# Wider runs in the first transform stage: nine runs of 512 columns for the first four rows, five runs for two later rows

## The chip, the cores and the metric

The kernel runs on one core of a Trainium2 chip. The metric is the device time of one execution in microseconds (us), as the median of several runs. When single instructions ran and how long they took is read from one profiled execution, whose times count from the start of its span.

## What is computed

The reference applies four layers to x of 2048 positions by 576 columns. Layers one and three mix by two Fourier matrices, layers two and four convolve and gate:

```python
x = x + _A_ref(_layernorm(x), seq_re, seq_im, hid_re, hid_im)
x = x + _B_ref(_layernorm(x), B_k, B_v, B_shift_k, B_ssm_k, B_ssm_D)
# _A_ref: y = Cr @ (x @ Wr) - Ci @ (x @ Wi)
# _B_ref: kv = shift_conv(k) * v;  y = q * (long_conv(kv, ssm_k) + kv * ssm_D)
```

The long convolution of kv with ssm_k does not depend on x, and both convolution layers use the same one. It is computed once, in several transform stages, beside the first mixing layer.

## The kernel before, in words

All products are made in float32r from a high and a low part: ScalarE (ACT) copies a tile into its rounded high part (L99, in `split`), VectorE (DVE) subtracts to get the low part (L100), and three of the four products of parts are summed on TensorE (PE).

**The main line.** The function `layer` runs the first mixing layer in steps. A step loads one 128 x 512 block of the Fourier matrix, splits it (`load_c`, L99 and L100, tile mats<-flts; called a c split here), and makes 14 matmuls of 512 columns: 12 into four banks s0 to s3 and two into the bank rm, which stand last. So the place in the program can be told by counting pairs of rm matmuls: the pair number n closes step n-1. In the first sixteen steps normalised rows of x are made too, on ACT, DVE and GpSimd (POOL).

**The first transform stage** is the generator `branch` (L351). The 2048 positions are 16 rows j of 128 partitions. A row has two items of 576 columns: source 1 is ssm_k as loaded, source 0 is the product kv. Source 0 comes from `convolve` (L384): for two rows together, DVE makes the shift convolution with multiplies and adds of 128 x 1152 (L395, L400); then L428 multiplies a row of it by v. An item is then split into f1r (L99 on ACT, tile f1r<-f1f for source 0 and f1r<-flts for source 1; L100 on DVE). The rows 0 to 3 (`K_FIRST`) keep a tile for each item; from row 4 on the two items of a row share a tile of 1152 columns, in which halves of 288 columns of source 0 and source 1 alternate.

A **run** (`f1_products`, L443) takes a stretch of columns of one such tile and makes six matmuls with the stage's constants: three products of parts, each for the upper and for the lower 64 partitions, which go to two banks. The weights there are 64 x 128, those of the main line 128 x 128. Three PSUM banks bf0, bf1, bf2 are handed out in turn (`turn`, L80), so a run shares one bank with the run before it. Behind the six matmuls ACT copies the two banks out (L453, here an eviction), and then issues one DMA that stores both halves to the tensor td in DRAM (L454). Rows 0 to 3 are 8 items with two runs of 288 columns each, 16 runs; each later row is three runs of 384 (`VW`), 36 runs.

**What sets the order.** `visits` is the list of runs that are due, each with the half step of the generator from which it may be emitted; `visit` emits at most one at a time. The loop around `layer` calls the generator at a pace that a table of numbers gives (`F1_16`, `F1_END`). A scheduler then puts the instructions of all engines into an order by its own model. On the chip every engine works through its own order and never passes an instruction that waits. The next stage (`bk<-mid`, L454's td as input) begins after the first stage's last stores, in step 45.

Of the kernel before, what the change touches and what calls it, by code (L numbers as in the profile page):

```python
# [12 lines left out]
AF = mybir.ActivationFunctionType  # L13
# [3 lines left out]
HP = P // 2  # L17
S = 2048
D = 576
J = S // P  # L20
TB = 4
NT = 512
HD = D // 2
# [7 lines left out]
ROWS = (0, 1, 2, 3, 4, 5, 6, 7, 8, 9)  # L31
K_FIRST = 4
F1_16 = 5
VW = 384
F1_END = 42
W_FROM = 41
HOLD = 125
# [14 lines left out]
WIDE = 2 * NT  # L52
# [14 lines left out]
def fnet_h3_kernel(ctx: ExitStack, tc: tile.TileContext, x, c_mat, w_re, w_im, k_pad, v, shift_k,  # L67
# [7 lines left out]
    def mm(ps, lhsT, rhs, first, last, more=False):  # L75
        return nc.tensor.matmul(ps, lhsT, rhs, start=first, stop=last, skip_group_check=more).ins  # L76
# [3 lines left out]
    def turn():  # L80
        given[0] += 1
        return banks[(given[0] - 1) % 3]
# [61 lines left out]
    def two(v):  # L144
        return v.rearrange("p (a n) -> p a n", a=2)
# [79 lines left out]
    W = {}  # L225

    def load_w():
        lay(flts, SC_AT + CRAW * NT + 4 * D, ("wl", D, 3))
# [122 lines left out]
    def branch():  # L351
        f1r = region_b(FR, "f1r")
        lay(f1r, 0, ("xf", 2 * D, 4), ("fc", 2 * P, 5))
        lay(f1r, 0, ("xp", 4 * D, 2))
        at = lay(flts, SC_AT + CRAW * NT, ("so", D, 4), ("land", D, 3))
        lay(flts, SC_AT + CRAW * NT, ("sp", 2 * VW, 3))
        lay(flts, at, ("craw", NT, 1))
        f1f = region_a(F32, "f1f")
        ks = f1f[:, :KR * 2 * D]
# [80 lines left out]
            parted[:] = split(h, l, two(r))  # L440
            return tuple(paired)

        def f1_products(j, fc, xf, at, n, so, to):  # L443
            ps = [turn()[:, :n] for _ in range(2)]
            last = seq[-1:]
            for k, (a, b) in enumerate(((0, 1), (0, 0), (1, 0))):
                for i in (1, 0):
                    half = slice(i * HP, (i + 1) * HP)
                    with behind(*last):
                        last = [mm(ps[i], fc[half, a, :], xf[b][half, at:at + n], k == 0, k == 2)]  # L450
            so = two(ring[so]())
            for i in range(2):
                stored[:] = [nc.scalar.activation(so[:, i, :], ps[i], AF.Copy).ins]  # L453
            nc.scalar.dma_start(t_d[:, j::J, to:to + n], so)  # L454

        conv, made_ops, visits = convolve(), 0, []
# [4 lines left out]
        for n, (j, src) in enumerate(todo):  # L461
            f1_loads(n + 1)
            if n < 2:
                yield
            xf = f1_split(j, src)
            if j < K_FIRST:
                visits += [(2 * n + 2, j, fcs[j], xf, hf * HD, HD, "so", hf * D + src * HD) for hf in range(2)]
            elif src:
                visits += [(2 * n + 3, j, fcs[j], xf, at, VW, "sp", at) for at in range(0, 2 * D, VW)]
            if n:  # L470
                f1_loads(n + 3)
            later = [m for m in range(n + 1, len(todo)) if todo[m][1] == 0 and 7 * (todo[m][0] // 2 + 1) > made_ops]
            for half in range(2):
                visit(2 * n + half)
                if later and n > 2:
                    left = 7 * (todo[later[0]][0] // 2 + 1) - made_ops
                    for _ in range(-(-left // (2 * (later[0] - n) - half)) if left > 0 else 0):
                        next(conv)
                        made_ops += 1
                yield  # L480
# [695 lines left out]
```

## Time and profile before

| what | value |
|---|---|
| median of three runs | 1181.65 us (1181.65 to 1184.18) |
| the profiled execution's own time | 1182.72 us |
| its span | 1180.9 us |
| ACT, busy | 650.9 us, 55% |
| POOL, busy | 75.5 us, 6% |
| evictions bf (L453) | 104, 43.2 us |
| stores td (L454) | 52 |

The profiled execution's time is 1.8 us above its span; this part lies outside of the trace. In rows of the trace the first number is the start or the stretch, the second the busy time; what stands in brackets is idle time of the engine ahead of the instruction, and what ended it. A row of several instructions (x6) runs from the first start to the last end. The matmuls overlap, so their distance in time is read from starts and not from lengths.

### The profile page before, as it was taken

To read this page: it belongs to the slowest core of one execution; us is meant where nothing else is said; L and a number is where in the kernel's file an instruction comes from. 1 tells how busy PE (TensorE), PEld (TensorE's weight loads), DVE (VectorE), ACT (ScalarE), POOL (GpSimd) and SP (SyncE) were. 2 spreads that over 40 slices of the span, in tenths; PEclk is the share of its full clock that TensorE was granted. 3 is DMA by queue.
4 is the path that set the end of the run, shared out by engine and by line. 5 is a ranking of instruction groups with operands and counts; after the bars stand their busy time and mean duration, and the time that the engine had idled before them with its cause. 6 is when DMAs were issued, how large, how long until landed. Compare 5 with 4: busy or idle time off the path is not lost.

```text
span 1180.9 us, 18086 instructions
## 1 busy us (share of the span) xinstructions
PE 1168.1 (99%) x6198; PEld 990.1 (84%) x6198; DVE 868.5 (74%) x1564; ACT 650.9 (55%) x1280; POOL 75.5 (6%) x115
## 2 busy tenths in 40 slices
PE   8999999999999999999999999999999999999997
PEld 6776667988888988888888898888888888889997
DVE  7899983788877778777757765965776776775764
ACT  7865655577766667766645666534434445450210
POOL 2310000000000000001101111000000000001111
PEclk9999999999999999999999999999999999999999
DMA  9879898545666656648966776862872787795621
GB/s 330 291 230 310 263 299 279 170 152 170 209 215 200 201 170 192 185 144 246 271 188 221 243 247 228 260 236 76 259 244 72 229 288 247 258 329 160 214 92 41
DMA packets 147453, 255.64 MB, mean 216 GB/s; under 512 B 16161, under 2 KB 56353, under 8 KB 147362
## 3 DMA queue, kind: packets, MB, share of 16 engines
q1 hardware_dynamic: 111890, 210.17, 55.7%
q10 hardware_dynamic: 28560, 37.91, 9.1%
q0 software_dynamic: 6912, 6.43, 2.4%
q8 instruction: 48, 0.79, 0.3%
q14 instruction: 43, 0.35, 0.1%
HBM read 187.80 MB, written 66.65 MB: 215 GB/s over the span
## 4 chain that ended last, share of the span: by engine, by line
PE 86%; DVE 5%; ACT 3%; DMA 3%; issue 2%; SPq 0%; ACTq 0%; POOL 0%; DVEq 0%
PE s L76 49%; PE bk L76 30%; PE rm L76 5%; PE bf L76 2%; DMA flts<-in_c_mat 1%; ACT flts L514 1%; DVE f1f L395 1%; DVE f1f L400 1%; DVE mats L100 1%; ACT mid L514 1%; DVE mid L520 1%; DMA early<-in_x 0%; ACT mats L99 0%; DMA yb<-flts 0%; DMA flts<-td 0%
## 5 line engine op out<-in xcount | busy, mean ns | idle before, releaser
L76 PE MATMUL s<-mats 128*128 128x512 f32 x2102 | 547.0, 396 | 3.9 <-DVE mats L761 1.5
L76 PEld LDWEIGHTS s<-mats 128*128 128x128 f32 x2102 | 383.7, 189 | 85.9 <-issue 11.1
L100 DVE TENSOR_TENSOR mats<-flts,mats 128x512 fp32r<-128x512 f32 x206 | 140.6, 687 | 50.5 <-ACT mats L99 48.9
L99 ACT ACTIVATE mats<-flts 128x512 fp32r<-128x512 f32 x206 | 128.2, 627 | 82.1 <-PE bk L76 31.6
L76 PE MATMUL bk<-mid 128*128 128x288 f32 x704 | 126.6, 301 | 1.5 <-ACT flts L514 0.8
L76 PEld LDWEIGHTS bk<-mid 128*128 128x128 f32 x704 | 108.7, 188 | 21.9 <-ACT flts L514 5.7
L514 ACT ACTIVATE flts<-bk 128x288 f32<-128x288 f32 (+1 forms) x192 | 76.5, 405 | 91.1 <-PE bk L76 76.0
L76 PE MATMUL bk<-w,u 128*128 128x288 f32 x864 | 120.4, 296 | 0.0
L76 PEld LDWEIGHTS bk<-w,u 128*128 128x128 f32 x864 | 117.4, 188 | 2.9 <-ACT flts L514 0.9
L520 DVE TENSOR_TENSOR mid<-flts,mid 128x576 fp32r<-128x576 f32 (+1 forms) x149 | 93.3, 627 | 19.1 <-ACT mid L514 16.3
L76 PE MATMUL rm<-mats 128*128 128x512 f32 x304 | 94.6, 391 | 0.2 <-ACT flts L514 0.2
L514 ACT ACTIVATE mid<-flts 128x576 fp32r<-128x576 f32 (+1 forms) x148 | 80.5, 576 | 9.8 <-DVE flts L535 5.1
L289 DVE TENSOR_TENSOR flts<-flts,bk 128x288 f32<-128x288 f32 x48 | 21.8, 454 | 68.3 <-PE bk L76 68.3
L76 PE MATMUL bk<-mats 128*128 128x288 f32 (+1 forms) x376 | 67.9, 317 | 0.0
L76 PEld LDWEIGHTS rm<-mats 128*128 128x128 f32 x304 | 57.0, 188 | 12.6 <-ACT flts L514 0.6
L453 ACT ACTIVATE flts<-bf 128x384 f32<-128x384 f32 (+1 forms) x104 | 43.2, 462 | 42.6 <-PE bf L76 39.8
L76 PE MATMUL s<-t,mats 128*128 128x512 f32 x264 | 64.9, 389 | 0.0
L186 POOL TENSOR_TENSOR flts<-flts 128x1 f32<-128x1 f32 x34 | 28.0, 823 | 516.4 <-DVE flts L185 514.0
L76 PE MATMUL bk<-mats,t 128*128 128x288 f32 (+1 forms) x368 | 59.3, 303 | 0.0
L514 ACT ACTIVATE flts<-flts 64x288 f32<-64x288 f32 x128 | 56.7, 443 | 4.5
L76 PEld LDWEIGHTS bk<-mats 128*128 128x128 f32 x376 | 55.5, 188 | 3.4
L76 PEld LDWEIGHTS s<-t,mats 128*128 128x128 f32 x264 | 49.6, 188 | 10.3
(152 smaller groups left out, 1495.5 us busy)
## 6 DMA issues: line engine op xcount, KB each, us to landing
flts<-in_c_mat SPq DMA_DIRECT2D x148, 256.0 KB, 3.6
ph<-in_c_mat SPq DMA_DIRECT2D x54, 512.0 KB, 4.1
flts<-in_c_mat SPq DMA_DIRECT2D x30, 512.0 KB, 5.7
flts<-td SPq DMA_DIRECT2D x53, 288.0 KB, 3.0
td<-flts ACTq DMA_DIRECT2D x36, 384.0 KB, 4.4
vd<-flts ACTq DMA_DIRECT2D x64, 144.0 KB, 2.5
flts<-vd SPq DMA_DIRECT2D x32, 288.0 KB, 3.9
ud<-ph ACTq DMA_DIRECT2D x12, 512.0 KB, 6.2
```

The costliest lines, as they stand in the source:

```text
L76: return nc.tensor.matmul(ps, lhsT, rhs, start=first, stop=last, skip_group_check=more).ins
L99: a = nc.scalar.activation(h, src, AF.Copy).ins
L100: return a, nc.vector.tensor_tensor(l, src, h.bitcast(F32), OP.subtract).ins
L186: pows.append(nc.gpsimd.tensor_tensor(rs, ve, mhalf, OP.pow).ins)
L289: added[:] = [nc.vector.tensor_tensor(r[:, cs], r[:, cs], ps[:, :HD], OP.add).ins]
L395: nc.vector.tensor_tensor(out_t[:, n], k, wt[3 - t][:, n], OP.mult)
L400: nc.vector.tensor_tensor(rp, rp, out_t, OP.add)
L453: stored[:] = [nc.scalar.activation(so[:, i, :], ps[i], AF.Copy).ins]
L514: last_act.append(nc.scalar.activation(*args, **kw).ins)
L520: nc.vector.tensor_tensor(l, src, h.bitcast(F32), OP.subtract)
```

## The change

Rows 0 to 3 no longer make two runs for each item. Their 8 x 576 columns are filled into runs of 512 one after the other, nine in all, and a run may so hold the end of one item and the start of the next (64 and 448, 128 and 384, and so on). For later rows two rows together, 2304 columns, make five runs of 464, 464, 464, 456 and 456; the third holds the last 224 columns of the even row and the first 240 of the odd row, which are of source 0 alone. A run that holds two pieces makes 12 matmuls, six for each piece, in the same two banks. The number of matmuls in the stage and the sum of their columns stay as they were; the number of runs goes from 52 to 39, that of the evictions from 104 to 78.

The stores change too. A store of rows 0 to 3 still takes both halves, but there is one for each piece and each half item: 24, not 16. In later rows each half is stored by itself, and each piece: 12 for two rows, not 6. Together 96, not 52. The output buffers become two of 1024 columns (so) and later five of 464 (sp) in place of four of 576 and three of 768. And the half steps at which runs are due change: an even row's first run is due one half step earlier.

```diff
-        def f1_products(j, fc, xf, at, n, so, to):
-            ps = [turn()[:, :n] for _ in range(2)]
-            last = seq[-1:]
+        def f1_products(pieces, so):
+            ps, last, at = [turn() for _ in range(2)], seq[-1:], 0
...
             for k, (a, b) in enumerate(((0, 1), (0, 0), (1, 0))):
-                for i in (1, 0):
-                    half = slice(i * HP, (i + 1) * HP)
-                    with behind(*last):
-                        last = [mm(ps[i], fc[half, a, :], xf[b][half, at:at + n], k == 0, k == 2)]
-            so = two(ring[so]())
+                for o, fc, xf, src, n in placed:
+                    for i in (1, 0):
+                        half = slice(i * HP, (i + 1) * HP)
+                        with behind(*last):
+                            last = [mm(ps[i][:, o:o + n], fc[half, a, :], xf[b][half, src:src + n],
+                                       k == 0 and o == 0, k == 2, o > 0)]
+            both = two(ring[so]()) if so == "so" else None
             for i in range(2):
-                stored[:] = [nc.scalar.activation(so[:, i, :], ps[i], AF.Copy).ins]
-            nc.scalar.dma_start(t_d[:, j::J, to:to + n], so)
+                one = ring[so]() if both is None else both[:, i, :]
+                stored[:] = [nc.scalar.activation(one[:, :at], ps[i][:, :at], AF.Copy).ins]
+                if both is None or i == 1:
+                    for (j, *_, to), (o, *_) in zip(pieces, placed):
+                        for n, cols in to:
+                            if both is None:
+                                nc.scalar.dma_start(t_d[:, j + i * J, cols:cols + n], one[:, o:o + n])
+                            else:
+                                nc.scalar.dma_start(t_d[:, j::J, cols:cols + n], both[:, :, o:o + n])
+                            o += n
...
-                visits += [(2 * n + 3, j, fcs[j], xf, at, VW, "sp", at) for at in range(0, 2 * D, VW)]
+                at, widths = (CUT[2], CUT[3:]) if j % 2 else (0, CUT[:2])
+                for i, w in enumerate(widths):
+                    visits.append((2 * n + 2 + j % 2 + i * (2 - j % 2), [(j, fcs[j], xf, at, w, [(w, at)])], "sp"))
+                    at += w
+                if at < 2 * D:
+                    open_run.append((j, fcs[j], xf, at, 2 * D - at, [(2 * D - at, at)]))
```

Line numbers of the changed kernel are higher: its evictions are L461, its stores L466 and L468, the high and low parts L100 and L101, the product with v L430, the convolution L397 and L402.

The scheduler's order moves at these places. The first is PE's order around its pair number 23 of rm matmuls, which ends step 22. Before, the last three runs ahead of it are those of row 4:

```order
L76 MATMUL bf1_67<-f1r_167 128x384
L76 MATMUL bf0_66<-f1r_167 128x384
L76 MATMUL s2_71<-mats_73 128x512 x3
L76 MATMUL s3_72<-mats_73 128x512 x3
L76 MATMUL rm_795<-mats_73 128x512 x2
L76 MATMUL s0_69<-mats_73 128x512
L76 MATMUL s1_70<-mats_73 128x512
```

Of the changed kernel, at the same pair of rm, with the last two matmuls of the run that joins rows 4 and 5 (224 and 240 columns) ahead of it, and the first two of row 5's run of 456 behind it:

```order
L77 MATMUL bf2_68<-f1r_167 128x240
L77 MATMUL bf1_67<-f1r_167 128x240
L77 MATMUL s0_69<-mats_73 128x512 x3
L77 MATMUL s1_70<-mats_73 128x512 x3
L77 MATMUL s2_71<-mats_73 128x512 x3
L77 MATMUL s3_72<-mats_73 128x512 x3
L77 MATMUL rm_790<-mats_73 128x512 x2
L77 MATMUL bf1_67<-f1r_167 128x456
L77 MATMUL bf0_66<-f1r_167 128x456
```

Ahead of this pair of rm stand 19 of the 52 runs before, and 12 of the 39 now. Of these 12, the first of row 4 (464 columns, both sources) stands 34 main matmuls and two more runs ahead of the end of the pair. The run of 456 writes bf1 first, which the joined run wrote too.

The second place is ACT's order there: the evictions of that joined run and what stands around them. Before, the item of row 6, source 0 (f1r<-f1f), stands ahead of the evictions of row 5's second run:

```order
L453 ACTIVATE flts_75<-bf0_66 128x384
L453 ACTIVATE flts_75<-bf2_68 128x384
L99 ACTIVATE mats_73<-flts_75 128x512
L454 DMA td_79<-flts_75 256x1x384
L99 ACTIVATE f1r_167<-f1f_168 128x2x288
L453 ACTIVATE flts_75<-bf1_67 128x384
L453 ACTIVATE flts_75<-bf2_68 128x384
```

In the changed kernel both items of row 6 stand ahead of the evictions (464 columns, bf2 and bf1) of the run that joins rows 4 and 5:

```order
L461 ACTIVATE flts_75<-bf0_66 128x464
L461 ACTIVATE flts_75<-bf2_68 128x464
L466 DMA td_79<-flts_75 128x464 x2
L100 ACTIVATE f1r_167<-f1f_168 128x2x288
L100 ACTIVATE f1r_167<-flts_75 128x2x288
L461 ACTIVATE flts_75<-bf2_68 128x464
L461 ACTIVATE flts_75<-bf1_67 128x464
L100 ACTIVATE mats_73<-flts_75 128x512
L466 DMA td_79<-flts_75 128x224
L466 DMA td_79<-flts_75 128x240
```

The two stores that end the piece come a second time, for the other half, and then the evictions of the run of 456. So ACT is now asked for row 6 ahead of the joined run's evictions, where it was asked ahead of those of row 5's second run before.

The third place is DVE's order just ahead of row 6's product with v. Before:

```order
L100 TENSOR_TENSOR f1r_167<-f1f_168,f1r_167 128x2x288
L395 TENSOR_TENSOR f1f_168<-f1f_168 128x1152
L100 TENSOR_TENSOR mats_73<-flts_75,mats_73 128x512
L100 TENSOR_TENSOR f1r_167<-flts_75,f1r_167 128x2x288
L400 TENSOR_TENSOR f1f_168<-f1f_168 128x1152
L100 TENSOR_TENSOR mats_73<-flts_75,mats_73 128x512
L428 TENSOR_TENSOR f1f_168<-f1f_168,flts_75 128x576
```

And of the changed kernel:

```order
L101 TENSOR_TENSOR f1r_167<-f1f_168,f1r_167 128x2x288
L397 TENSOR_TENSOR f1f_168<-f1f_168 128x1152
L101 TENSOR_TENSOR mats_73<-flts_75,mats_73 128x512
L101 TENSOR_TENSOR f1r_167<-flts_75,f1r_167 128x2x288
L402 TENSOR_TENSOR f1f_168<-f1f_168 128x1152
L397 TENSOR_TENSOR f1f_168<-f1f_168 128x1152
L430 TENSOR_TENSOR f1f_168<-f1f_168,flts_75 128x576
```

Counted from the end of step 15's evacuation (u<-flts) to this product, the changed order has one c split less and one operation of the convolution more; the rest of the operations are the same. Behind step 44 the orders of all engines agree.

More of the change, by code (lines that the diff above doesn't have):

```diff
@@ L227, in load_w @@
     def load_w():
-        lay(flts, SC_AT + CRAW * NT + 4 * D, ("wl", D, 3))
+        lay(flts, SC_AT + CRAW * NT + OUT_END, ("wl", D, 3))
         wg = region_a(FR, "w").rearrange("p (k n) -> p k n", k=9)
@@ L354, in branch @@
         lay(f1r, 0, ("xp", 4 * D, 2))
[L355 to L356 removed]
+        lay(flts, SC_AT + CRAW * NT, ("so", WIDE, 2))
+        at = lay(flts, SC_AT + CRAW * NT + OUT_END, ("land", D, 3))
+        lay(flts, SC_AT + CRAW * NT, ("sp", CUT[0], 5))
         lay(flts, at, ("craw", NT, 1))
@@ L466, in branch @@
             if j < K_FIRST:
-                visits += [(2 * n + 2, j, fcs[j], xf, hf * HD, HD, "so", hf * D + src * HD) for hf in range(2)]
-            elif src:
-                visits += [(2 * n + 3, j, fcs[j], xf, at, VW, "sp", at) for at in range(0, 2 * D, VW)]
+                at = 0
+                while at < D:
+                    w = min(NT - filled(), D - at)
+                    cut = [max(at, HD * hf) for hf in range(2)], [min(at + w, HD * (hf + 1)) for hf in range(2)]
+                    open_run.append((j, fcs[j], xf, at, w, [(hi - lo, lo % HD + hf * D + src * HD)
+                                                            for hf, (lo, hi) in enumerate(zip(*cut)) if lo < hi]))
+                    at += w
+                    if filled() == NT:
+                        visits.append((2 * n + 2, list(open_run), "so"))
+                        open_run.clear()
+            elif not src and j % 2:
+                open_run.append((j, fcs[j], xf, 0, CUT[2], [(CUT[2], 0)]))
+                visits.append((2 * n + 3, list(open_run), "sp"))
+                open_run.clear()
+            elif src:
+                at, widths = (CUT[2], CUT[3:]) if j % 2 else (0, CUT[:2])
+                for i, w in enumerate(widths):
+                    visits.append((2 * n + 2 + j % 2 + i * (2 - j % 2), [(j, fcs[j], xf, at, w, [(w, at)])], "sp"))
+                    at += w
+                if at < 2 * D:
+                    open_run.append((j, fcs[j], xf, at, 2 * D - at, [(2 * D - at, at)]))
             if n:
```

11 lines of the change are left out of this document (9 added, 2 removed).

## The prediction

> **What bounds the kernel now.** I read the page first, then the chain of work that ended last for the first 230 us, then the busy times in stretches of 20 us, then the timelines of PE, ACT and DVE where they meet.
>
> ```profile
> PE 1168.1 (99%) x6198; PEld 990.1 (84%) x6198; DVE 868.5 (74%) x1564; ACT 650.9 (55%) x1280; POOL 75.5 (6%) x115
> ```
>
> PE is busy all the time, so what shortens PE's own work should shorten the kernel, as long as PE doesn't wait. The chain says where it nearly does:
>
> ```profile
> 74.69 2.48 PE s L76 x10
> 78.34 1.27 DVE f1f L400
> ...
> 116.03 1.15 DVE f1f L400
> 117.44 1.13 issue
> 121.06 0.80 PE bf L76 x6
> ```
>
> From 78 to 117 us the chain runs over DVE's convolution and not over PE. In the stretches, the columns after the length are busy PE, PEld, DVE and ACT:
>
> ```profile
> 20.00:40.00 20.00, 20.00 (x99) 15.23 (x99) 17.13 (x46) 18.94 (x39) 3.78 (x5) 1.00 0.99 364
> 40.00:60.00 20.00, 20.00 (x96) 15.35 (x95) 17.55 (x35) 17.14 (x39) 6.89 (x4) 1.00 0.70 238
> 60.00:80.00 20.00, 20.00 (x100) 14.99 (x98) 18.86 (x28) 13.31 (x28) 2.58 (x4) 1.00 0.72 215
> 80.00:100.00 20.00, 20.00 (x103) 14.59 (x102) 20.00 (x24) 10.10 (x22) 1.58 (x3) 1.00 0.88 281
> 100.00:120.00 20.00, 20.00 (x102) 13.65 (x101) 20.00 (x24) 10.92 (x23) 1.06 (x2) 1.00 0.98 330
> ```
>
> DVE has no idle time at all from 80 to 120 us. The change takes nothing from DVE. So two engines bound this stage, and a gain on PE counts only where DVE has already delivered.
>
> **What a run costs PE.** The change makes fewer, wider runs with as many matmuls and columns. What a run costs beside its columns can be read from starts:
>
> ```profile
> 198.54 2.72 PE s L76 x12
> ...
> 78.46 0.68 PE L76 MATMUL bf<-f1r 64*128 64x288 f32 x6
> 79.07 0.96 PE L76 MATMUL s<-mats 128*128 128x512 f32 x3
> 79.95 0.66 PE L76 MATMUL bf<-f1r 64*128 64x288 f32 x6
> ...
> 146.88 0.79 PE L76 MATMUL bf<-f1r 64*128 64x384 f32 x6
> 147.60 1.66 PE L76 MATMUL s<-mats 128*128 128x512 f32 x6
> 149.19 0.79 PE L76 MATMUL bf<-f1r 64*128 64x384 f32 x6
> ```
>
> Twelve main matmuls in the chain take 2.72 us, 0.227 each. From one run of 288 to the next are 1.49 us with three main matmuls between (0.68), so the run costs 0.81. For 384 it is 2.31 less six (1.36), 0.95. The two widths differ by 3 x 96 columns (upper and lower halves run side by side) and by 0.14 us, 0.00049 us a column; so 0.39 us of each run is for getting into the 64-row weights and out again. Runs of 512, 464 and 456 then cost 1.14, 1.07 and 1.06.
>
> All runs of before: 16 x 0.81 + 36 x 0.95 = 47.2 us. After: 9 x 1.14 = 10.2; six pairs of rows at 3 x 1.07 + 2 x 1.06 = 5.33 each, 32.0. Short pieces add something that no row shows. At least it is nothing; at most a pair of matmuls waits for its weights, which come in three pairs in 0.43 us (row below), 0.14 a pair, where 64, 128 and 192 columns alone need 0.03, 0.06 and 0.09. For two pieces of each width and three products that is at most 1.4; I take 0.7, in the middle. One run of rows 0 to 3 is cut in two by main matmuls, 0.4. Sum 43.3: **3.9 us less work on PE**.
>
> ```profile
> 63.06 0.43 PEld L76 LDWEIGHTS bf<-f1r 64*128 64x128 f32 x6 [0.35 <-issue]
> ```
>
> [...]
>
> **Where PE will wait.** What decides is the last place at which PE is held by another engine; from there on the time is PE's remaining work. I find this place at the end of step 22, the 23rd pair of rm. Before, that pair had been issued by 99.4 us, and step 23 began at 99.45:
>
> ```profile
> 0.00:99.40 99.40, 14.33 (x46) 8.64 (x46) 0.67 (x1) 0.60 (x1) 1.00 0.85 282
> ...
> 99.45 1.46 PE L76 MATMUL s<-mats 128*128 128x512 f32 x5
> ```
>
> In the changed order the next on PE is row 5's run of 456. It needs bank bf1, so the second eviction of the run that joins rows 4 and 5. On ACT these evictions stand behind both items of row 6, and the first of them needs row 6's product from DVE. This wait has a small precedent in the profile of before:
>
> ```profile
> 119.17 0.74 DVE L428 TENSOR_TENSOR f1f<-f1f,flts 128x576 f32<-128x576 f32 x1
> 119.94 0.69 ACT L99 ACTIVATE f1r<-f1f 128x576 fp32r<-128x576 f32 x1 [0.41 <-DVE f1f L428]
> 120.53 0.47 ACT L453 ACTIVATE flts<-bf 128x384 f32<-128x384 f32 x1
> 121.06 0.80 PE L76 MATMUL bf<-f1r 64*128 64x384 f32 x6 [0.47 <-ACT flts L453]
> ```
>
> ACT waited 0.41 us for a product, an eviction stood behind it, and PE waited 0.47 for the bank. For row 6, the rows of before are:
>
> ```profile
> 98.18 1.34 DVE L395 TENSOR_TENSOR f1f<-f1f 128x1152 f32<-128x1152 f32 x1
> 99.45 0.67 DVE L100 TENSOR_TENSOR mats<-flts,mats 128x512 fp32r<-128x512 f32 x1
> 100.05 0.74 DVE L100 TENSOR_TENSOR f1r<-flts,f1r 128x576 fp32r<-128x576 f32 x1
> ...
> 102.59 0.74 DVE L428 TENSOR_TENSOR f1f<-f1f,flts 128x576 f32<-128x576 f32 x1
> ...
> 103.37 0.69 ACT L99 ACTIVATE f1r<-f1f 128x576 fp32r<-128x576 f32 x1 [0.29 <-DVE f1f L428]
> 103.96 0.85 ACT L453 ACTIVATE flts<-bf 128x384 f32<-128x384 f32 x2
> ```
>
> The product ended at 103.33 (102.59 + 0.74). The changed order has one c split less ahead of it (0.60, from starts) and one convolution operation more (1.27): 104.0. ACT starts 0.04 later, makes two items at 0.59 from start to start (103.37 to 103.96), and two evictions, 0.85 for 384 columns and so about 1.03 for 464. **PE gets the bank at about 106.3**, 6.8 later than PE came to this place before.
>
> But less is left to do then. Before, 33 of the 52 runs stood behind this place, 33 x 0.95 = 31.4. Now 27 of 39: two of 456 and five pairs of rows, 2.1 + 26.7 = 28.8. That gives back 2.6. Two small terms cancel. The wait of 0.47 at 121 us goes, since PE is later there. And the run of 456 has four stores of one piece each between its bank and its evictions. A store of 128 partitions and one half is nearest to vd's, 0.33 to issue; with both halves it took 0.52:
>
> ```profile
> L550 ACTq DMA_DIRECT2D vd<-flts x64: 326/326/362, 223.4 to 539.2; - x64
> ...
> L454 ACTq DMA_DIRECT2D td<-flts x52: 520/521/788, 10.9 to 197.7; - x52
> ```
>
> Four take 1.3 to 2.1 us, nearer to 1.3. From 106.3, the evictions of the run of 456 end at 106.3 + 1.3 + 1.0 = 108.6 to 109.4; the next run wants its bank after 1.06 us and six main matmuls (1.36), at 108.7. So it waits nothing to 0.7 us; I take 0.5. Later evictions stand on ACT behind products that DVE has made by then, as the order shows, and behind step 44 nothing differs.
>
> The sum: 6.8 - 2.6 - 0.5 + 0.5 = **+4.2 us**, or 1186.9 on the profiled execution's own 1182.72. That execution is 1.07 above the median of the runs shown, 1181.65; on the median it is **1186** (1185.9). What the runs save ahead of step 22 doesn't enter, nor do the wider evictions: they only let PE come earlier to a place where it waits.
>
> [...] It is ACT's order, not its load, that I charge for.
>
> **The rivals.**
>
> *DVE comes earlier, and PE keeps its gain* (not slower). DVE is idle for 2.9, 2.5 and 1.1 us in the three stretches from 20 to 80 us. A part of it is waiting for POOL's power:
>
> ```profile
> DVE flts L688 <- POOL flts L655: 1.6, 3, 0.7
> ```
>
> If the new order covers these waits, row 6's product comes earlier, each microsecond gives one back, and at 4.2 the kernel is as fast as before. If DVE came still earlier, PE would be held by nothing and all 3.9 of its work would be gained: 1177.8 on the median. Against it: the changed order puts the dependent row right behind these waits in about as many places, and ACT, 18.94 busy of 20 from 20 to 40 us, leaves no room. Chance 0.18, of which 0.12 for the full gain.
>
> *ACT's block costs nothing.* If the evictions weren't held (a product that comes some 3 us early on ACT, or another bank), PE would still be held at row 4's first run, which stands 34 main matmuls and two runs ahead of our place, and which needs both items of row 4:
>
> ```profile
> 91.77 0.74 DVE L100 TENSOR_TENSOR f1r<-flts,f1r 128x576 fp32r<-128x576 f32 x1
> ...
> 92.86 0.79 PE L76 MATMUL bf<-f1r 64*128 64x384 f32 x6
> ```
>
> They were ready at 92.5, and PE used them at 92.86. With one c split less ahead of them in the changed order (0.60) they are ready at 91.9; then 34 x 0.227 + 3 x 1.07 = 10.9 gives 102.8, 3.4 later than before. Less 2.6, it is +0.8: 1182.4. For it speaks that the same place is then held by one thing only, against it the order rows, which are plain. Chance 0.15.
>
> *The stores hold the loads* (slower still). 96 stores in place of 52 are issued, and a load on SP's queue has waited for a store before:
>
> ```profile
> SPq L169 <- DMA td<-flts: 3.4, 1, 3.4
> ```
>
> One such wait more, where a c split has no slack, adds 3.4: 1189.3. The stretch from 100 to 120 us already shows a DMA share of 0.98. Chance 0.12.
>
> **How the numbers follow.** The forecast has 0.55, with 1184 to 1188 by its unknown terms (the product 1 us earlier or later, the stores 0.7, evictions). A measurement of this kernel can tell about 0.3%, 3.5 us, from no change, so faster is below 1178.1 and slower above 1185.2. Of the forecast 0.40 lies above that and 0.15 within; the first rival gives 0.12 faster and 0.06 within; the second 0.13 within and 0.02 slower; the third 0.12 slower. That makes 0.12 faster, 0.34 the same, 0.54 slower. The range of 8 in 10 leaves out the full gain and what lies beyond one held load: 1179.0 to 1190.5.
>
> **What would show it.** PE's rows should show idle time ahead of row 4's first run of 464 (released by DVE f1r) and about 3 us ahead of the first run of 456 behind the 23rd pair of rm (released by ACT's eviction), with ACT idle ahead of f1r<-f1f and released by L430 near 104 us. From 130 us on PE should be later than before by some 6 us less 0.4 for each pair of rows done, and from step 44 on by a constant 4 us. If PE's idle time there is below 1 us, the first rival is right; if c splits hold PE, with SP's queue waiting for td, the third. Wrong would be the whole argument if DVE were idle between 75 and 105 us, or if a run cost less than 0.3 us beside its columns.

## The result and the profile after

The changed kernel takes **1198.47 us** (median of four runs, 1197.79 to 1199.78), the kernel before 1181.65 in the same comparison: 16.8 us slower, ratio 1.014 (95% interval 1.0125 to 1.0155). The prediction was 1186.0, with a range up to 1190.5. The sign was right; the loss is four times as large.

Lines of the changed kernel differ from those of before: the product is L430 now, the splits L100 and L101, the evictions L461, the stores of later rows L466. Profiled was an execution of 1199.78 us; its span is 1198.0, 17.1 more than before. The page's first row, and then stretches of 20 us (columns as in the prediction):

```profile
PE 1169.7 (98%) x6198; PEld 990.8 (83%) x6198; DVE 870.8 (73%) x1564; ACT 647.6 (54%) x1254; POOL 73.8 (6%) x115
```

```profile
60.00:80.00 20.00, 17.29 (x83) 12.75 (x83) 17.05 (x29) 12.85 (x24) 1.60 (x3) 1.00 0.51 145
80.00:100.00 20.00, 17.60 (x90) 12.44 (x88) 20.00 (x24) 7.57 (x13) 1.58 (x3) 1.00 0.92 280
100.00:120.00 20.00, 16.53 (x79) 11.51 (x80) 17.79 (x20) 10.03 (x19) 1.05 (x2) 0.91 0.82 260
...
140.00:160.00 20.00, 19.24 (x101) 13.56 (x100) 11.99 (x16) 12.56 (x24) 1.05 (x2) 1.00 0.71 228
160.00:180.00 20.00, 16.15 (x78) 11.20 (x75) 19.97 (x25) 9.23 (x18) 0.53 (x1) 0.91 0.83 266
```

Two things are new here. PE, which was busy all the time before, now has idle time in each of them. And the granted clock, 1.00 in every such stretch of before, is 0.91 in two of them. PE's waits from 14 to 225 us, first of before, then of the change (total, times, longest):

```profile
PE s L76 <- ACT mats L197: 1.4, 1, 1.4
PE bf L76 <- ACT flts L453: 0.5, 1, 0.5
```

```profile
PE bf L77 <- ACT flts L461: 9.4, 6, 3.9
PE bf L77 <- DVE f1r L101: 2.4, 3, 1.0
PE s L77 <- ACT mats L198: 2.4, 2, 2.2
PE s L77 <- DVE mats L101: 1.8, 3, 1.4
PE s L77 <- ACT mats L100: 1.1, 1, 1.1
```

PE has 17.1 us of waits in place of 1.9; more than half of it is for evictions. The timeline at the place that the prediction names, and ahead of it:

```profile
100.70 1.01 ACT L461 ACTIVATE flts<-bf 128x464 f32<-128x464 f32 x2 [3.45 <-DMA td<-flts]
...
101.31 1.39 PE L77 MATMUL bf<-f1r 64*128 64x464 f32 x6 [2.28 <-ACT flts L461]
...
102.99 0.76 DVE L101 TENSOR_TENSOR f1r<-f1f,f1r 128x576 fp32r<-128x576 f32 x1 [2.18 <-ACT f1r L100]
...
108.74 0.75 DVE L430 TENSOR_TENSOR f1f<-f1f,flts 128x576 f32<-128x576 f32 x1
...
109.44 0.61 PE L77 MATMUL rm<-mats 128*128 128x512 f32 x2
...
109.53 0.68 ACT L100 ACTIVATE f1r<-f1f 128x576 fp32r<-128x576 f32 x1 [5.68 <-DVE f1f L430]
...
110.69 0.99 ACT L461 ACTIVATE flts<-bf 128x464 f32<-128x464 f32 x2
...
111.73 0.92 PE L77 MATMUL bf<-f1r 64*128 64x456 f32 x6 [1.68 <-ACT flts L461]
```

The chain is the forecast one: product (L430), ACT idle for 5.68 us until it comes, two items, two evictions, and PE's run of 456 behind them. Nothing on ACT passes the item that waits: the joined run's last matmul started at 106.38 us, and its evictions start at 110.69. But the product ends at 109.49 and not at 104.0. PE had done its main matmuls by 110.05, 10.6 us later than before, so this chain itself costs it 1.68 us; the rest of its delay was there already. Above the chain stands a wait that the prediction doesn't have: an eviction that waits 3.45 us until an earlier store has landed, because its output buffer is still being read (`e9` below takes another buffer, and the wait is gone). PE waits 2.28 us behind that eviction, and DVE 2.18 behind an item that ACT could only make after it.

A second such place follows at step 34, where the prediction expects none:

```profile
151.50 0.99 ACT L461 ACTIVATE flts<-bf 128x456 f32<-128x456 f32 x2 [1.45 <-DMA td<-flts]
...
153.05 0.69 DVE L101 TENSOR_TENSOR mats<-flts,mats 128x512 fp32r<-128x512 f32 x1 [4.14 <-ACT mats L100]
...
166.64 0.75 DVE L430 TENSOR_TENSOR f1f<-f1f,flts 128x576 f32<-128x576 f32 x1
...
167.42 0.68 ACT L100 ACTIVATE f1r<-f1f 128x576 fp32r<-128x576 f32 x1 [4.99 <-DVE f1f L430]
...
169.62 1.40 PE L77 MATMUL bf<-f1r 64*128 64x456 f32 x6 [3.85 <-ACT flts L461]
```

Here DVE isn't short of time: it is busy 11.99 of 20 us from 140 to 160. It stands still for 4.14 us behind a c split whose high part stands on ACT behind four evictions, with the 1.45 us for a landing among them; so its next product is late, ACT waits 4.99 for it, and PE 3.85 for the evictions of the joined run behind it.

The clock, in stretches of 5 us around both places:

```profile
100.00:105.00 5.00, 3.69 (x12) 2.58 (x13) 2.82 (x4) 3.10 (x6) 0.00 (x0) 0.66 0.82 279
...
165.00:170.00 5.00, 1.15 (x6) 0.67 (x6) 5.00 (x7) 2.58 (x5) 0.00 (x0) 0.98 0.72 213
170.00:175.00 5.00, 5.00 (x21) 3.19 (x20) 5.00 (x6) 1.13 (x4) 0.00 (x0) 0.68 0.75 214
```

Behind the wait of 2.28 us the clock is granted at 0.66 on average, and behind that of 3.85 at 0.98 and 0.68: 0.34 x 5 = 1.7 us lost in each case, on top of the wait.

How late PE is against before, by the start of each step (counted by the pairs of rm in both timelines): step 10 -0.1 us, step 16 +3.4, step 20 +5.5, step 22 +12.2, step 23 +13.1, step 28 +10.9, step 34 +12.7, step 35 +18.4, step 44 +15.7.

### The profile page after: what moved, and what is told of

It is laid out like the page before. It is cut to its first block, busy times and chain, and to the rows that moved or that the text cites. A ratio compares the mean times of both kernels' runs of the same rounds, so it can differ in the third digit from the quotient of the medians.

```text
span 1198.0 us, 18132 instructions
## 1 busy us (share of the span) xinstructions
PE 1169.7 (98%) x6198; PEld 990.8 (83%) x6198; DVE 870.8 (73%) x1564; ACT 647.6 (54%) x1254; POOL 73.8 (6%) x115
## 4 chain that ended last, share of the span: by engine, by line
PE 74%; ACT 2%; DVE 2%; DMA 2%; issue 1%; ACTq 0%; DVEq 0%; SPq 0%
PE s L77 42%; PE bk L77 28%; PE rm L77 4%; ACT flts L551 1%; DMA yb<-flts 1%; ACT mid L551 1%; DMA flts<-in_c_mat 0%; DVE mid L557 0%; ACT mats L100 0%; DMA flts<-td 0%; DVE u L101 0%; DVE mats L101 0%; ACT u L100 0%; DVE flts L571 0%; DVE flts L570 0%
## 5 line engine op out<-in xcount | busy, mean ns | idle before, releaser
L101 DVE TENSOR_TENSOR mats<-flts,mats 128x512 fp32r<-128x512 f32 x206 | 140.9, 688 | 62.7 <-ACT mats L100 61.9
L100 ACT ACTIVATE mats<-flts 128x512 fp32r<-128x512 f32 x206 | 128.1, 626 | 85.6 <-PE bk L77 31.2
L551 ACT ACTIVATE mid<-flts 128x576 fp32r<-128x576 f32 (+1 forms) x148 | 80.5, 576 | 10.1 <-DVE flts L572 5.1
L77 PEld LDWEIGHTS rm<-mats 128*128 128x128 f32 x304 | 57.0, 188 | 12.3
L461 ACT ACTIVATE flts<-bf 128x464 f32<-128x464 f32 (+2 forms) x78 | 39.7, 559 | 41.7 <-PE bf L77 25.0
L77 PEld LDWEIGHTS s<-t,mats 128*128 128x128 f32 x264 | 49.5, 188 | 10.3
```

The lines of the kernel that those rows point to most:

```text
L100: a = nc.scalar.activation(h, src, AF.Copy).ins
L101: return a, nc.vector.tensor_tensor(l, src, h.bitcast(F32), OP.subtract).ins
L461: stored[:] = [nc.scalar.activation(one[:, :at], ps[i][:, :at], AF.Copy).ins]
L551: last_act.append(nc.scalar.activation(*args, **kw).ins)
```

## The experiments

The expectations call the theories by letters. A: the order on ACT in the later rows, with the items of the next row ahead of the joined run's evictions. B: the filled runs of rows 0 to 3 make steps 8 to 16 late. C: stores, that is buffers that are not free yet and the number of stores. D: DVE's late products. Differences are medians against the kernel before in the same comparison, whose own median moves between 1181.65 and 1183.42 us; differences of one or two us between two experiments are therefore not told apart. Most of these edits also move the scheduler's orders. Only `e9` leaves PE's and DVE's as they were; elsewhere a difference is that of the edit and of its new order together.

### One half of the change alone

`e1_only_first` has the nine runs for rows 0 to 3 and the old later rows; `e2_only_later` the old rows 0 to 3 and the new later rows.

```diff
 # e1, against the change
-            elif not src and j % 2:
...
+                visits += [(2 * n + 3, [(j, fcs[j], xf, at, VW, [(VW, at)])], "sp") for at in range(0, 2 * D, VW)]
...
 # e2, against the change
-                at = 0
-                while at < D:
...
+                visits += [(2 * n + 2, [(j, fcs[j], xf, hf * HD, HD, [(HD, hf * D + src * HD)])], "so") for hf in range(2)]
```

> Rows 0 to 3 in nine runs of 512 as in the change; the later rows as before (three runs of 384 for a row, one store for both halves, three output buffers of 768, the half steps of before). Theory A, ACT's order in the later rows (the items of the next row, which wait for DVE's product, stand on ACT ahead of the evictions of the joined run) makes the loss: about as before, 1180 to 1183 us. Theory B, the wide runs of rows 0 to 3 make DVE and the c splits late in steps 8 to 16 (PE was 3.4 us late at step 16), and that is carried on: 1185 us or more. Theory C, the stores of the later rows, 72 in place of 36, hold buffers and loads: as theory A here, since these stores are those of before.

> Rows 0 to 3 as before (16 runs of 288, four output buffers of 576); the later rows in five runs for two rows as in the change. Theory A: nearly the whole loss, 1193 to 1198 us, with ACT idle ahead of f1r<-f1f (released by L430) and PE waiting for the eviction behind it. Theory B: 4 to 6 us less than the changed kernel, 1192 to 1194, and PE on time at step 16. Theory C: 1193 or more, with evictions that wait for a store to land as the main idle time of ACT.

Measured: 1193.47 (+10.5) and 1192.32 (+9.3). Each half loses about ten, and together they don't lose twenty; so neither A nor B is the whole, and the losses don't add. In `e2` PE is 0.7 us early up to step 21, then 2.3 late at step 23 and 10.8 late at step 35. Its second place, in the timeline and in stretches of 5 us:

```profile
158.52 0.76 DVE L430 TENSOR_TENSOR f1f<-f1f,flts 128x576 f32<-128x576 f32 x1
...
159.31 0.68 ACT L100 ACTIVATE f1r<-f1f 128x576 fp32r<-128x576 f32 x1 [4.99 <-DVE f1f L430]
...
161.51 0.74 PE L77 MATMUL bf<-f1r 64*128 64x456 f32 x2 [4.31 <-ACT flts L461]
```

```profile
155.00:160.00 5.00, 2.20 (x16) 1.47 (x14) 5.00 (x7) 0.69 (x2) 0.53 (x1) 0.94 0.79 225
160.00:165.00 5.00, 3.49 (x11) 2.50 (x12) 5.00 (x8) 2.97 (x6) 0.00 (x0) 0.50 0.68 212
165.00:170.00 5.00, 5.00 (x23) 3.52 (x22) 4.41 (x6) 2.56 (x5) 0.00 (x0) 0.87 0.92 317
```

The same 4.99 us as in the change, with rows 0 to 3 as before. PE waits 4.31 us, and the clock takes another 3.4 (0.06, 0.50 and 0.13 of 5).

### ACT's order changed

`e3_behind` and `e4_later_behind` put all item splits of later rows behind the evictions emitted so far, in the change and in `e2`; `f3_later_even0` (in `e2`) and `f4_after_even0` (in the change) only the source-0 items of rows 6, 8 and so on.

```diff
-            xf = f1_split(j, src)
+            with behind(*(stored if j >= K_FIRST else ())):                               # e3, e4
+            with behind(*(stored if j > K_FIRST and j % 2 == 0 and not src else ())):     # f3, f4
+                xf = f1_split(j, src)
```

> The change, with the item splits of the later rows put behind the evictions that have been emitted so far (order alone; same instructions, stores and buffers). Theory A: both blocks go (about 5 us at steps 20 to 22 and 5 us at step 34), 1186 to 1190 us. Theory B alone: 1195 to 1198, since the lateness from steps 8 to 16 stays and only its place changes. Theory C alone: 1195 or more, the evictions still wait for stores to land.

> Rows 0 to 3 as before, the later rows as in the change but with their item splits behind the emitted evictions. If theories A and B together make the whole loss, nothing of it is left, and the six runs fewer give 0.4 us each: 1179 to 1182 us. If theory C has a part of its own (store landings that hold evictions), 1185 or more.

> As the second run (rows 0 to 3 as before, later rows as in the change), with the source-0 items of rows 6, 8, ... put behind the evictions that have been emitted, so behind those of the joined run; source 1 and the odd rows stay. Theory A: the 4.3 us of PE's wait at the joined run's bank near 157 us and the half clock behind it go, 1185 to 1188. If another wait takes its place, as when all items were moved: 1191 to 1195.

> The same move alone in the change itself. Theory A: the waits of 1.7 and 3.9 us behind the two joined runs and one half-clock stretch go, 1189 to 1193 us. If another wait takes their place: 1195 to 1199.

Measured: 1196.18 (+13.2), 1194.46 (+11.5), 1190.03 (+7.2) and 1201.74 (+18.9). Moving all items takes two to four us from the change and nothing from `e2` (11.5 and 9.3, with intervals that overlap): there an item is then made so late that PE waits for it.

```profile
132.31 0.75 DVE L101 TENSOR_TENSOR f1r<-flts,f1r 128x576 fp32r<-128x576 f32 x1
...
133.17 1.14 PE L77 MATMUL bf<-f1r 64*128 64x464 f32 x4 [4.20 <-issue]
```

The narrow move of `f3` does at its place what A says: at step 35 PE is 3.8 us late, not 10.8. Some 20 us on, this comes in its stead:

```profile
178.83 1.60 ACTq L466 DMA_DIRECT2D td<-flts  x3
...
180.53 0.99 ACT L461 ACTIVATE flts<-bf 128x456 f32<-128x456 f32 x2 [1.92 <-DMA flts<-in_w_im]
...
181.58 0.89 PE L77 MATMUL bf<-f1r 64*128 64x456 f32 x6 [1.97 <-ACT flts L461]
```

```profile
180.00:185.00 5.00, 3.42 (x14) 2.58 (x15) 0.96 (x2) 3.50 (x7) 0.00 (x0) 0.82 0.92 327
185.00:190.00 5.00, 5.00 (x22) 3.55 (x21) 1.19 (x3) 1.67 (x4) 0.00 (x0) 0.84 0.61 164
```

A wait of 1.97 us and 1.7 of clock (0.18 and 0.16 of 5). The time lies between the two that the expectation gave, 1185 to 1188 and 1191 to 1195. The same move in the change gains nothing: there PE is 12.9 late at step 35, not 18.4, and 16.9 again at step 40. A is shown as what holds PE at the joined runs, and it falls as the account of the loss: without it, most of the loss is still there.

### Output buffers and stores

`e5_before_shallow` gives the kernel before fewer buffers and changes nothing else. `e6_after_pairs2` and `g2_later_pairs2` store both halves at once from two pairs of buffers, in the change and in `e2`. `e8_after_deep` gives the change deeper buffers from the words of a landing buffer, and `e7_after_nocraw` is its control. `g1_before_88` gives the kernel before as many stores in the later rows as the change has. `e9_rotate` hands the five buffers out in another order, and `e10_rotate_behind` adds that to `e3`.

```diff
 # e5, against before
+        lay(flts, SC_AT + CRAW * NT, ("so", D, 2))
...
+        lay(flts, SC_AT + CRAW * NT, ("sp", 2 * VW, 2))
 # e6 (and g2), against the change (and e2)
+        lay(flts, SC_AT + CRAW * NT, ("sp", 2 * CUT[0], 2))
...
+            both = two(ring[so]())
 # e7 and e8
-        lay(flts, at, ("craw", NT, 1))
...
 # e8 alone
+        lay(flts, SC_AT + CRAW * NT, ("so", WIDE, 3))
+        lay(flts, SC_AT + CRAW * NT, ("sp", CUT[0], 6))
 # e9 and e10
+        ring["sp"].tiles[:] = ring["sp"].tiles[3:] + ring["sp"].tiles[:3]
 # g1, against before
+            for i in range(2) if n == VW else ():
+                nc.scalar.dma_start(t_d[:, j + i * J, to:to + n], so[:, i, :])
...
```

> The kernel before with as few output buffers as the change leaves: two (not four) for rows 0 to 3, two pairs (not three) for later rows, so that evictions have four buffers where the change has four and then five. Nothing else is changed. Theory C, depth (an eviction waits until the store of the run two before it has landed, and ACT passes nothing): a third of the loss or more, 1187 us or more, with evictions that wait for td. Theories A and B, the order of the later rows' items and the shape of the wide runs: about as before, 1181 to 1184.

> The change with one store for both halves of each piece in the later rows, 42 stores in all and not 96, from two pairs of buffers of 464 and not five single ones. If the number of stores counts (issue on ACT, or their share of the queue): 1192 to 1196 us. If the depth of the buffers counts: no faster than the change, 1198 to 1203. If neither: 1197 to 1199.

> Control for the next one: the change without the third landing buffer for blocks of the Fourier matrix, which gives 512 words free. Some microseconds slower than the change, 1199 to 1206, since the blocks are loaded later.

> The change without that third landing buffer, its words used for three pairs of 512 for rows 0 to 3 and six single output buffers for the later rows. Theory C, depth: 4 to 8 us less than the control without the deeper buffers. Theories A and B: within 2 us of the control.

> The change with its five single output buffers handed out in another order (the fourth first), so that the first run of the later rows doesn't write over the buffer of the run just before it but over that of the run before that. PE's and DVE's orders stay as they are. Theory C, landings: the 3.4 us for which ACT waited there for a store go, with PE's 2.3 us behind them and the half clock that followed; 1193 to 1196 us. Theory A: the product of row 6 is then awaited in its place, 1197 to 1199.

> The same order of buffers, and the item splits of the later rows behind the emitted evictions as in the third run. If landings and ACT's order each have a share of their own: 1189 to 1193 us. If DVE's products are what everything waits for in the end, whichever wait comes first: 1194 to 1196, no better than either alone.

> The kernel before, with each half of the later rows' runs stored by itself: 72 stores in place of 36 there, 88 in all. Runs, buffers and due times stay. If the number of stores counts by itself (issues on ACT that wait for earlier landings, with evictions and c splits behind them): 1186 to 1192 us, later only from step 20 on. If it does so only beside the joined runs and the fewer buffers: 1181 to 1185.

> As the second run (rows 0 to 3 as before, later rows as in the change), with one store for both halves of each piece from two pairs of buffers of 464: 18 stores for two halves in place of 36 for one. If the number of stores counts: 1185 to 1189 us. If fewer buffers take back what fewer stores give: 1190 to 1194, with evictions that wait for td.

Measured: `e5` 1198.39 (+15.4); `e6` 1197.00 (+14.0); `e7` 1218.99 and `e8` 1214.01 (+36.0 and +31.0; in `e8` the third landing tile shares words with the buffer of rm's rest, so some items hold other values); `e9` 1199.34 (+15.9); `e10` 1197.23 (+13.8); `g1` 1184.09 (ratio 1.0009, 0.9999 to 1.0019); `g2` 1187.60 (+4.5). The stores are 60 in `e6`, not the 42 expected; in `g2` 36 for two halves stand in place of 72 for one. `e7` was expected at 1206 us at most. `e10` is no better than `e3` alone.

Depth is worth much where it is scarce. ACT's waits from 14 to 205 us in `e5`, and then in `g2`:

```profile
ACT flts L454 <- DMA td<-flts: 42.9, 21, 5.4
```

```profile
ACT flts L461 <- DMA td<-flts: 18.4, 10, 3.9
```

In the kernel before it was 2.6 us, once; in the change 10.5 us, seven times. So `e5` shows that fewer buffers alone can cost the kernel before as much as the whole change does. `e8` is 5.0 us below its control, with intervals that overlap a little. But landings don't account for the change: with 23.3 us of such waits on ACT `e6` is no slower than the change, and in `g2` ACT waits more for landings than in `e2` (4.2), and is 4.7 us faster. What is different in `g2` is read in its order on ACT: the scheduler itself puts the source-0 item behind the joined run's evictions at step 34. No wait of PE for an eviction is longer than 1.2 us, and the clock is 1.00 throughout the stage. The number of stores by itself costs the kernel before nothing measurable (`g1`).

`e9` is the cleanest single step. PE's and DVE's orders are the same as in the change, and the wait of 3.45 for a landing is gone. The product then ends at 108.11 and not 109.49, and PE gets its bank 1.4 us earlier:

```profile
107.36 0.75 DVE L430 TENSOR_TENSOR f1f<-f1f,flts 128x576 f32<-128x576 f32 x1
...
108.14 0.68 ACT L100 ACTIVATE f1r<-f1f 128x576 fp32r<-128x576 f32 x1 [4.84 <-DVE f1f L430]
...
110.34 1.13 PE L77 MATMUL bf<-f1r 64*128 64x456 f32 x4 [2.65 <-ACT flts L461]
```

So at this place PE's time is the product's time plus 2.2 us, as forecast. DVE has no idle time left between the end of step 15 and the product, 30.8 us later, which is what the prediction reckons (73.2 to 104.0); it starts 0.9 us later than in the change, so that of the 2.18 us 1.4 are seen. But the end doesn't move: PE now waits 2.65 us in one piece there, with 1.7 us of clock behind it, as in the change behind the wait of 2.28, and is 18.9 us late at step 35. In all the clock costs 6.8 us in this execution and 3.4 in the change's; 1.7 of that is behind a wait at 15 us, ahead of everything that this edit touches, and so is chance.

### Rows 0 to 3 in other runs

`e11_first384` fills rows 0 to 3 into 12 runs of 384 with the three pairs of buffers of before; `e12_first_due` is `e1` with its runs due a half step later.

```diff
 # e11, against e1
-        lay(flts, SC_AT + CRAW * NT, ("so", WIDE, 2))
+        lay(flts, SC_AT + CRAW * NT, ("so", 2 * VW, 3))
...
-                    w = min(NT - filled(), D - at)
+                    w = min(VW - filled(), D - at)
...
 # e12, against e1
-                        visits.append((2 * n + 2, list(open_run), "so"))
+                        visits.append((2 * n + 3, list(open_run), "so"))
```

> Rows 0 to 3 filled together into 12 runs of 384 and not 9 of 512, with the three pairs of output buffers of the kernel before for all rows; the later rows as before. Theory C, depth: 1179 to 1184 us, four runs fewer than before at 0.4 us each and no wait for a buffer. Theory B, any run filled across items of rows 0 to 3 upsets the order of steps 8 to 16: 1188 to 1194, as with nine runs.

> As the first run (rows 0 to 3 in nine runs of 512, later rows as before), with the nine runs due one half step later. Theory B as a matter of where the scheduler puts these runs: 1184 to 1189 us, with less waiting of PE in steps 8 to 16. If their place doesn't matter (the late DVE or the shallow buffers do it): 1191 to 1196.

Measured: 1193.80 (+10.4) and 1194.24 (+10.8), as `e1`. So the loss needs neither the width of 512, nor the shallow buffers, nor the half step. In `e12` PE is 1.5 us late at step 16, not 4.1 as in `e1`, and yet 12.0 late at step 23, where `e1` is 12.8. In `e11` no eviction waits for td at all; this holds PE instead:

```profile
83.34 0.68 ACT L101 ACTIVATE f1r<-flts 128x576 fp32r<-128x576 f32 x1 [3.88 <-DMA flts<-in_ssm_k]
...
83.93 0.85 ACT L462 ACTIVATE flts<-bf 128x384 f32<-128x384 f32 x2
...
84.83 0.44 PE L78 MATMUL bf<-f1r 64*128 64x384 f32 x2 [4.16 <-ACT flts L462]
```

It is the same form once more: an item on ACT that waits, this time for a load, with the eviction behind it that PE needs.

### DVE made lighter

In `f1_light_before` and `f2_light_after` the convolution's adds work on 32 of each 576 columns.

```diff
-                        nc.vector.tensor_tensor(rp, rp, out_t, OP.add)
+                        nc.vector.tensor_tensor(rp[:, :, :32], rp[:, :, :32], out_t[:, :, :32], OP.add)
```

> The kernel before, with the convolution's three adds for two rows done on 32 of each 576 columns only (the other columns of rp stay without them), which takes some 1.1 us of DVE for each add, 27 us over the stage. PE has only 1.9 us of waits there, so by every theory: 1179 to 1182 us. This is the base of the next run.

> The change with the same cut in the convolution's adds (32 of each 576 columns). ACT's order in the later rows is that of the change, items of even rows ahead of the joined run's evictions. Theory D, DVE's late products are what the blocks consist of: the loss goes and the saving of the runs shows, 1175 to 1181 us, 2 to 4 less than the run before it. Theory C, landings of stores and shallow buffers: 6 us or more above the run before it, 1186 or more.

Measured: 1182.01 and 1192.26. The kernel before gains nothing measurable from a lighter DVE (ratio 0.9993, 0.9983 to 1.0003), the change some 6 us: `f2` stands 10.3 above `f1`, the change 16.8 above the kernel before. At the first place nothing is held by the product any more, as the stretch from 100 us shows. The landing ahead of it still is waited for (3.69 us on ACT, and 1.99 on PE at 98.39), and the second place is as it was:

```profile
100.00:120.00 20.00, 20.00 (x110) 14.31 (x108) 15.10 (x23) 10.37 (x20) 1.05 (x2) 1.00 0.93 311
```

```profile
145.18 0.69 DVE L101 TENSOR_TENSOR mats<-flts,mats 128x512 fp32r<-128x512 f32 x1 [4.28 <-ACT mats L100]
...
158.56 0.68 ACT L100 ACTIVATE f1r<-f1f 128x576 fp32r<-128x576 f32 x1 [3.99 <-DVE f1f L430]
...
160.76 0.47 PE L77 MATMUL bf<-f1r 64*128 64x456 f32 x2 [2.99 <-ACT flts L461]
```

So D accounts for the product at the first place and, with the new order, for about 6 us in all, and not for the second place, where DVE, with time to spare, stands 4.28 us behind ACT.

### What the loss consists of

The sum of PE's waits from 14 to 225 us, the time lost at a lower clock (worked out from stretches of 5 us) and the saved work (3.9 us for the change as in the prediction, 0.39 a run for a half of it), each against before, make most of the difference of the spans (`f2` stands against `f1`):

| kernel | waits | clock | saved | sum | span |
|---|---|---|---|---|---|
| the change | +15.2 | +3.4 | -3.9 | +14.7 | +17.1 |
| e1 | +7.9 | +5.1 | -2.7 | +10.3 | +11.8 |
| e2 | +10.1 | +3.4 | -2.3 | +11.2 | +11.3 |
| e5 | +11.1 | +3.4 | 0 | +14.5 | +15.5 |
| f2 | +9.2 | +3.4 | -3.9 | +8.7 | +9.4 |
| f3 | +8.3 | +1.7 | -2.3 | +7.7 | +9.0 |
| g2 | +6.2 | 0 | -2.3 | +3.9 | +6.5 |

A part of what is left lies behind the stage: in the change PE waits another 1.05 us at 229 us for DVE, and is 16.9 us late behind that (in `e2`, `f2` and `f3` the same wait falls into the window); in `g2`, 4.1 late at step 44, 2.3 us come only after 784 us. The rest, about 1 us each way, isn't accounted for.

The first of PE's waits, near 14 us, is 2.1 to 2.7 us long in all twelve kernels with filled runs in rows 0 to 3, and 1.2 to 1.4 in the other eight. In seven of the twelve profiled executions 1.7 us of clock follow it, in the change's own none.

## Why the prediction was wrong

**Two engines bound the stage, and a saving on PE counts only where DVE has delivered.** Half right. DVE wasn't enough: with a lighter DVE the saving still didn't show. What delivers to PE's runs is ACT, which stands between both, and the prediction looked at its order in one place only.

**A run costs 0.39 us beside its columns, 3.9 us in all.** Nothing speaks against it. From a run's start to the next main matmul were 0.61 us for 288 columns and 0.72 for 384 before; in the change a run of 464 takes 0.83:

```profile
196.22 0.90 PE L77 MATMUL bf<-f1r 64*128 64x464 f32 x6
197.05 3.01 PE L77 MATMUL s<-mats 128*128 128x512 f32 x12
```

The steps are 0.11 and 0.11, those of the prediction 0.14 and 0.12. In the trace of before the 0.39 lies at the two ends of a run: by medians of its 14 unbroken runs of 288, from a main matmul to the run's first pair are 0.32 us and from one main matmul to the next 0.23; from the first pair to the second 0.24 and from the second to the third 0.13; from the third to the main matmul 0.22, and from that to the next 0.34. That is 0.09, 0.10, 0.09 and 0.11 more, 0.40 in all. No run measures the saving by itself; by the sums above and below it is there, and is spent several times over.

**The deciding place, and 6.8 us at it.** The place and the chain were right, and from product to bank it took 2.2 us where 2.3 were forecast. What failed is "104.0", and with it the time at which PE comes to the place: the product ended at 109.49, and PE got its bank at 111.73, 12.3 us later than it had come there before, not 6.8. The prediction took DVE's time from the trace of before and corrected it by one operation and one split. DVE was 3.2 us late by the end of step 15:

```profile
73.18 0.68 DVE L100 TENSOR_TENSOR u<-flts,u 64x512 fp32r<-64x512 f32 x1 [0.70 <-ACT u L99]
```

```profile
76.41 0.68 DVE L101 TENSOR_TENSOR u<-flts,u 64x512 fp32r<-64x512 f32 x1 [0.70 <-ACT u L100]
```

And it stood still for 2.18 us at 101 us, behind the landing that ACT waited for. That is 5.4 of the 5.5, and it is what the prediction itself named as the end of its argument: DVE idle between 75 and 105 us. That a landing and ACT make those 2.18 is shown by `e9`, where they are gone. But the product is not all. PE itself came to the place at 110.05, 10.6 us late, where the second rival's sum has 3.4; from 14 us on it had waited 10.0 us (1.4 before) and lost 1.7 by the clock. The wait that it named for row 4's first run is there (0.81 us for DVE at 95.19), but it is one of ten. So the block that the prediction prices cost 1.68 us there, not some 3, and that the sign came out right is more luck than reckoning. What made DVE late in steps 8 to 16 is read from the trace only (PE, ACT and DVE wait for one another there in a new order), and `e11` and `e12` show what the loss doesn't need.

**The store issues, 1.3 to 2.1 us, and 0.5 of wait behind them.** Right: 1.89 us and 0.48.

**"Later evictions stand on ACT behind products that DVE has made by then, as the order shows."** This is the second step that failed. An order shows what stands behind what, and not when it is ready. At step 34 the product was 5 us late, since DVE had itself stood behind ACT; from step 34 to 35 PE lost 5.7 us.

**What comes ahead of step 22 doesn't enter.** Wrong in a way that wasn't thought of. The saving didn't show, but DVE's delay and PE's own waits did.

**A wait costs what it lasts.** This was taken for granted, and two waits cost 1.7 us more each by the clock.

**The saving in what is left to do, 2.6 us.** It does come in between the places (13.1 us late at step 23, 10.9 at step 28; 18.4 at step 35, 15.7 at step 44). From the bank at 111.73 to step 44 PE lost 7.2 us by waits and clock, 0.5 before, and became only 3.4 us later; so some 3.2 us were saved, an estimate from these numbers.

**Behind step 44 nothing differs.** The orders agree, but PE's 1.05 us of wait at 229 us has no counterpart before: 15.7 us late at step 44 become 16.9.

Of the rivals, the stores didn't hold the loads to any effect: from 14 to 205 us the loads on SP's queue (L170, and L169 before) wait 4.1 us for td, 5.2 before, and no c split on ACT waits longer than 0.5 us for a load. The full gain is excluded by the time. So is the second rival's 1182.4, though the block was nearly as cheap as it says. It stays open how the 16.8 us divide. The two halves lose 10.5 and 9.3 alone; each wait that an experiment took away brought another further on; and no version with filled or joined runs came nearer to the kernel before than 4.5 us.

## What to carry to other kernels

Where three engines hand work round with no slack, follow the engine in the middle: for each wait on it, write down what stands behind it, and date both from the new order, not from the old trace; a delay of one engine moves every date after it. If one such block is found, look for the next one of the same form before the sum is made, and add to a wait of PE what the clock costs behind it: here 1.7 or 3.4 us behind 18 of 19 waits from 2.39 us up, and 1.7 us behind 12 of 22 from 1.67 to 2.28 us.

## What the runs showed of the hardware

The clock is lost in portions. Behind PE's waits in all twenty profiled executions, but for their last 7 us, the time lost, by windows of half a microsecond, is nothing, 1.7 us or 3.4 us, at half the clock for 3.4 or 6.8 us. By themselves, waits of up to 1.52 us never brought it; of 22 waits from 1.67 to 2.28 us 12 did; of 19 from 2.39 us up 18 (two waits in `e5`, 0.5 us apart, are counted as one of 5.02 us). Two waits of 2.18 us at the same place, in the change and in `e1`, differ: without and with. The wait of 1.97 us in `f3` cost 1.7 us more.

A store's issue on ACT can itself wait for a load. In the change a store issue starts at 136.36 us, 0.02 us after a load of v on SP's queue has landed, and two more start at 125.69 and 130.35 us, 0.02 us after a load of v and one of k. In the trace each of these stores waits for the landing semaphore of that load (104, 103 and 108) and has the same one for its own landing. The eviction behind the first has waited 3.93 us and is put down to the load of v, which it doesn't read. In `f3` an eviction stands behind three store issues, which take 1.60 us from 178.83 us; its wait of 1.92 us is put down to in_w_im, which it doesn't read either. On ACT a wait for landings therefore isn't only a matter of the buffer.
